# A two-layer linear-attention transformer on one core: the second layer's output weights spaced out, its attention chain moved up

## The chip, the core and the metric

The kernel runs on one core of one Trainium2 chip. The metric is the device time of one launch in microseconds, as the median of several runs. The engines are TensorE (PE; its weight loads are PEld), VectorE (DVE), ScalarE (ACT), GpSimd (POOL) and SyncE (SP), which issues most of the DMAs.

## The reference

A stack of four blocks works on x of 2048 x 576: attention, feed-forward, attention, feed-forward, with the same weights both times.

```python
x = x + A(layernorm(x))       # 32 heads of 18: phi = [softmax(p), softmax(-p)] with p = head @ w_phi,
                              # o = phi_q (phi_k^T v) / (phi_q . sum(phi_k) + 1e-6), then o @ wo
x = x + B(layernorm(x))       # relu(x @ w1 + b1)**2 @ w2 + b2, width 4608
x = x + A(layernorm(x))
x = x + B(layernorm(x))
```

All is float32. The kernel keeps that precision by splitting each matmul operand into a high and a low part and adding three products.

## The kernel before

The 2048 rows are worked in four blocks of 512 (0 to 3), and a block's feed-forward (`g_mlp`) is one **stage**. A stage runs over 36 slices of the hidden width. One slice is one **unit**: the hidden product H(f) (L955, 14 matmuls into `m_*ph`), relu and square on ACT (L960, L961), a cast and a subtraction on DVE that give the two parts `m_*hb` (L964, L965), and the second product S(f) (L980 and L972, 15 matmuls into `m_*acc`). On PE the order is H(f), S(f-1), H(f+1), S(f). The weights of a unit come from memory on SP's queue: `m_*h` (640 KB, for H) and `m_*s` (576 KB, for S), each with two buffers, so that the load of H(f+1) can go out when H(f-1) has ended.

Beside a stage runs the attention of the block that comes next (`plan_attend`). In the second layer the blocks come in the order 1, 0, 3, 2: block 0's attention (tiles `a_0*`) runs beside stage 1 (`m_1*`), block 3's beside stage 0, block 2's beside stage 3. For a block, the steps are:

- projections of the queries (`a_*qp`, L498) from activations fetched back from memory (`a_*uh`, `a_*ul`, L485); block 0 has its queries already,
- for each of four row tiles the softmaxes on DVE and ACT (L534 to L571), a rearrangement on POOL, a store to memory (L737), a fetch of it in another layout (L742, on ACT's queue), and a **flip**: a transpose in blocks on DVE (L747),
- ten copies in two parts (`pieces`, L756 and L757) and ten `times` steps of three matmuls each (`a_*pn`, L776),
- the output weights in four **pieces** o0h, o0l, o1h, o1l (L315 on SP, each as two DMAs of 126 and 72 rows). They go into the buffers of the fetched tiles (tag names `wraw` and `rr`), so they must wait for the last copies out of these,
- the projections with them (`a_*po`, L799), one row tile after another, then the norm, stored, fetched and flipped in the same manner for the next stage.

The order of all this is a table: `plan.put(turn, depth, call)` puts a call into a slot, two slots to a unit, and `weave` takes one slot after each H and one after each S. PE, ACT, DVE and POOL keep the order so written; the order on SP's queue is set by the framework's scheduler from when it thinks an operand is there. Every queue runs in order: an instruction that waits holds those behind it.

Of the kernel before, what the change touches and what calls it, by code (L numbers as in the profile page):

```python
# [21 lines left out]
def layers_kernel(  # L22
# [23 lines left out]
    out = out.rearrange("o s d -> (o s) d")  # L46
# [8 lines left out]
    NG = (H + HG - 1) // HG  # L55
# [39 lines left out]
    def weave(main, other, rate):  # L95

        due = 0.0
        for _ in main:
            due += rate
            while due >= 1.0 and next(other, other) is not other:  # L100
                due -= 1.0
        drain(other)
# [204 lines left out]
    def asked(which, name, tags=TAGS_A):  # L307

        pair, calls = [], []

        def ask(half, k):
            if k == 0:
                pair.append(piece_tiles(f"{name}{which}{half}", tags))
            for d, piece in moved(which, half, k, pair[half][k]):
                nc.sync.dma_start(piece, d)  # L315

        return pair, [lambda half=half, k=k: ask(half, k) for half in range(2) for k in range(2)]
# [163 lines left out]
    def unspill(b, x, i, name):  # L481
        if not x:
            x.update(xt_tiles(name))
        d, piece = xt_part(b, x, i)
        nc.sync.dma_start(piece, d)  # L485
# [38 lines left out]
    def make_raw(x, t, pair, name):  # L524
        raw = new_raw(t, name)
        for half in range(2):
            half_raw(x, t, pair, half, raw, name)
        return raw
# [280 lines left out]
    def plan_norm(plan, norm, x_of, stats, scales, turns, rests, late=()):  # L809
        for t in range(NT):  # L810
            plan.put(stats[t], 0, lambda t=t: norm.stats(t, x_of(t)))
            plan.put(scales[t], 1, norm.scale, t)
            plan.put(turns[t], -1 if t in late else 2, norm.turn, t)
        for h in range(2):
            plan.put(rests[h], 2, norm.rest, h)

    def plan_queries(plan, at, gap, layer, raws, er, ph, name):

        zb = sums[layer]["zb"]
        r = {}  # L820

        def first(t):
            if t == 0:
                r[0] = sb.tile([P, NT, 2, H], F32, tag="rq", name=f"{name}r", bufs=1)
            er.append(exponents(raws[t], f"{name}Q{t}"))

        def second(t):
            e, rt = er[t], r[0][:, t]
            totals(e, rt)
            m = sb.tile([P, 2, D], F32, tag="m", name=f"{name}m{t}", bufs=1)  # L830
            u = sb.tile([P, 2, H], F32, tag="u", name=f"{name}u{t}", bufs=1)
            nc.vector.tensor_mul(m, e, zb)
            nc.vector.tensor_reduce(u, m.rearrange("p s (h d) -> p s h d", d=DH), op=ALU.add, axis=AX.X)
            r[t + 1] = u

        def third(t):
            e, rt, u = er[t], r[0][:, t], r.pop(t + 1)
            nc.vector.tensor_mul(u, u, rt)
            nc.vector.scalar_tensor_tensor(u[:, 0], u[:, 0], DEN_EPS, u[:, 1], op0=ALU.add, op1=ALU.add)
            nc.vector.reciprocal(u[:, 1], u[:, 0])  # L840
            nc.vector.tensor_mul(rt, rt, u[:, 1].unsqueeze(1).to_broadcast([P, 2, H]))
            scaled(e, rt)
            ph.append(e)

        for t in range(NT):
            plan.put(at + gap * t, 0, first, t)
            plan.put(at + gap * t + 1, 1, second, t)
            plan.put(at + gap * t + 2, 2, third, t)
        return at + gap * (NT - 1) + 2

    def plan_attend(plan, at, gap, layer, b, raws, dst, name, o, queries=None):

        out = Out(layer, b, [], name)
        out.pair, calls = o
        if queries:
            for t in range(NT):
                plan.put(at + gap * t, 0, queries, t)
            at += 1
        if layer == 0:
            for n, call in enumerate(calls):  # L860
                plan.put(at + n, 9, call)
        done = at + 2
        at = plan_queries(plan, at, gap, layer, raws, [], out.ph, name) + 1
        if layer:
            for t in range(NT):
                for k, (step, call) in enumerate(((0.5, out.arrange), (1.5, out.store), (2.5, out.fetch), (4, out.flip))):
                    plan.put(done + gap * t + step, -1, call, t)
            at += 3.5
        for i in range(2 * NG):
            plan.put(at + i / 2, 0, out.pieces if layer else out.turn, i)  # L870
            plan.put(at + (i + 1 + layer) / 2, 1, out.times, i)
        if layer:
            for n, call in enumerate(calls):
                plan.put(at + NG + n / 4, 9, call)
            at += 1.5
        at += NG + 1
        for t in range(NT):
            plan.put(at + t - 1, 9, out.load, t)
        trips = range(NT) if layer else range(NT - 1)
        norm = TripNorm(dst, f"{name}n", b, out.keep, trips, layer == 1)  # L880
        more = 0 if queries else 2
        scales = [at + 1, at + 2, at + 3, at + 4 if layer else at + 5.5 + more]
        turns = [at + more + k for k in (4, 5, 6.5, 7)]
        for t in trips:
            plan.put(scales[t] + 0.5, -1, norm.store, t)
            plan.put(at + more + t + 2.5, -1, norm.fetch, t)
            plan.put(at + more + (3.5, 4.5, 6, 6.5)[t], -1, norm.flip, t)
        plan_norm(plan, norm, out.project, [at + t for t in range(NT)], scales, turns, [at + 5 + more, at + 7 + more])
# [538 lines left out]
    def body():  # L1427

        order = [NB - 1, NB - 2] + list(range(NB - 2))
        queries, other, o, last_keys = opening()  # L1430
        for layer in range(2):
            q1 = None
            ready, prev_rows, keep = {}, None, {}
            for i, b in enumerate(order):
                n = f"{layer}_{b}"
                nxt, rows = {}, []
                gen = g_mlp(layer, b, ready, rows, f"m{n}", layer == 0 and i == 0, i == 0, layer == 1 and i == NB - 1)
                plan = Plan()
                if i == 0:
                    out = Out(layer, b, [], f"t{layer}o")  # L1440
                    out.pair = o[0]
                    barrier(layer, b, last_keys, queries, other, ready, out, gen)
                    for t in range(NT):
                        plan.on(2 + t, 0, out.keep, t, out.x[t])
                at = 0
                if prev_rows is not None:
                    at = plan_keys(plan, prev_rows, i == NB - 1, keep)
                if i + 1 < NB:
                    nb, n2 = order[i + 1], f"a{layer}_{order[i + 1]}"
                    if i or layer:  # L1450
                        o = asked("o", n2, TAGS_C)
                    if i == 0:
                        plan_attend(plan, 1, 3, layer, nb, [other.raws[t] for t in range(NT)], nxt, n2, o)
                    else:
                        raws2, held = [], {}
                        start, step = (at - 4, 0.5) if at else (0, 0.75)
                        for k in range(4):
                            plan.put(start + 2 * step * k, -2, lambda k=k, held=held, nb=nb, n2=n2:
                                     unspill(nb, held, k, f"{n2}u"))
                        if q1 is None or not layer:  # L1460
                            q1, calls = asked("q", n2)
                            for call, k in zip(calls, (1, 3, 6, 7)):
                                plan.put(start + step * k, -3, call)
                        plan_attend(plan, at or 6.5, 2, layer, nb, raws2, nxt, n2, o,
                                    lambda t, held=held, q1=q1, raws2=raws2, n2=n2:
                                    raws2.append(make_raw(held, t, q1, f"{n2}q")))
                weave(gen, plan.slots(), 1.0)
                ready = nxt
                if layer == 0:
                    prev_rows = (b, rows)  # L1470
            if layer == 0:
                queries, other, o, last_keys = between(rows, keep)
                order = [order[-1], order[-2]] + order[:2]
# [43 lines left out]
    with tc.manual_schedule(engines=ordered):  # L1517
        body()
# [22 lines left out]
```

## Time and profile before

| | |
|---|---|
| Median of three runs | 2523.01 us (2520.92 to 2524.05) |
| The profiled execution | 2526.71 us, of which its span 2525.0 us |
| PE busy | 2495.7 us, 99% of the span |
| DVE, ACT, POOL busy | 1223.7, 769.7 and 152.5 us |
| DMA | 540.99 MB, 214 GB/s in the mean |
| TensorE's granted clock | 0.996 in the mean |

PE is busy nearly throughout; the other engines and the DMA work in its shadow, and count where PE waits for them. The page's table of waits and the timelines around them tell where that is.

### The profile page before, as it was taken

What the parts mean: (1) busy time and instruction counts of PE and PEld (TensorE: products, weight loads), DVE (VectorE), ACT (ScalarE), POOL (GpSimd) and SP (SyncE); (2) the same over time, 40 slices, a digit from 0 to 9 for tenths busy, and PEclk for the clock granted to TensorE, in tenths of its full rate; (3) what the DMA queues carried; (4) which work ended last, traced back from release to release, by engine and by line L of the source; (5) the groups of instructions that cost most, each with busy time, mean ns of one, the idle gap of its engine ahead of it and who ended that gap; (6) DMA issues with size and microseconds to landing.
All of it is one profiled execution on the core that took longest, in us unless ns stands there. A gap on an engine that the chain in (4) does not pass through costs nothing.

```text
span 2525.0 us, 37453 instructions
## 1 busy us (share of the span) xinstructions
PE 2495.7 (99%) x15084; PEld 2198.6 (87%) x15084; DVE 1223.7 (48%) x2115; ACT 769.7 (30%) x1358; POOL 152.5 (6%) x419
## 2 busy tenths in 40 slices
PE   9999999999999999999999999999999999999999
PEld 8998888898888988888889988788887888888887
DVE  6887955444635446355114776433463426433112
ACT  5544443322222222223223332313223222312221
POOL 4302000000000000000000011000010002000000
PEclk9999999999999999999999999999999999999999
DMA  9514888867648576484564348668575767667665
GB/s 318 175 53 135 288 279 283 307 230 268 215 157 288 179 255 207 165 292 146 193 196 158 130 139 268 215 196 281 177 254 181 259 225 239 206 204 247 197 195 171
DMA packets 196619, 540.99 MB, mean 214 GB/s; under 512 B 26270, under 2 KB 79390, under 8 KB 196446
## 3 DMA queue, kind: packets, MB, share of 16 engines
q1 hardware_dynamic: 163806, 511.06, 60.8%
q10 hardware_dynamic: 32640, 27.53, 3.4%
q8 instruction: 120, 1.97, 0.3%
q14 instruction: 53, 0.43, 0.0%
HBM read 440.12 MB, written 98.40 MB: 213 GB/s over the span
## 4 chain that ended last, share of the span: by engine, by line
PE 97%; DMA 2%; DVE 1%; ACT 0%; issue 0%; SPq 0%; DVEq 0%; ACTq 0%
PE m_2ph L955 9%; PE m_0ph L955 9%; PE m_1ph L955 9%; PE m_3ph L955 9%; PE m_2acc L980 7%; PE m_1acc L980 7%; PE m_3acc L980 7%; PE m_0acc L980 7%; PE m_2acc L972 2%; PE m_1acc L972 2%; PE m_0acc L972 2%; PE m_3acc L972 2%; PE a_0po L799 1%; PE a_2po L799 1%; PE kvp L598 1%; PE a_3po L799 1%
## 5 line engine op out<-in xcount | busy, mean ns | idle before, releaser
L955 PE MATMUL m_0ph<-a_0nh,m_0h 128*128 128x512 f32 x720 | 226.8, 397 | 5.6 <-DMA m_0h<-dw 5.6
L955 PE MATMUL m_2ph<-a_2nh,m_2h 128*128 128x512 f32 x720 | 225.4, 395 | 0.0
L980 PE MATMUL m_1acc<-m_1s,m_1hb 128*128 128x448 f32 x864 | 189.0, 367 | 0.4 <-PE m_1ph L955 0.4
L980 PE MATMUL m_2acc<-m_2s,m_2hb 128*128 128x448 f32 x864 | 189.3, 367 | 0.0
L980 PE MATMUL m_3acc<-m_3s,m_3hb 128*128 128x448 f32 x864 | 188.9, 367 | 0.3 <-DVE m_3hb L964 0.3
L980 PE MATMUL m_0acc<-m_0s,m_0hb 128*128 128x448 f32 x864 | 189.0, 367 | 0.0
L964 DVE CAST m_2hb<-m_2hr 128x512 fp32r<-128x512 f32 x72 | 30.8, 427 | 311.1 <-ACT m_2hr L961 310.7
L980 PEld LDWEIGHTS m_1acc<-m_1s,m_1hb 128*128 128x128 f32 x864 | 161.9, 188 | 18.7 <-PE m_1ph L955 0.5
L980 PEld LDWEIGHTS m_3acc<-m_3s,m_3hb 128*128 128x128 f32 x864 | 161.2, 188 | 17.4 <-PE m_3ph L955 0.5
L980 PEld LDWEIGHTS m_2acc<-m_2s,m_2hb 128*128 128x128 f32 x864 | 160.9, 188 | 16.1
L980 PEld LDWEIGHTS m_0acc<-m_0s,m_0hb 128*128 128x128 f32 x864 | 160.5, 188 | 15.4
L955 PEld LDWEIGHTS m_0ph<-a_0nh,m_0h 128*128 128x128 f32 x720 | 136.1, 189 | 37.4 <-issue 6.2
L964 DVE CAST m_0hb<-m_0hr 128x512 fp32r<-128x512 f32 x72 | 30.8, 428 | 273.4 <-ACT m_0hr L961 273.0
L955 PEld LDWEIGHTS m_2ph<-a_2nh,m_2h 128*128 128x128 f32 x720 | 135.3, 188 | 30.4
L960 ACT ACTIVATE m_0hr<-m_0ph,b1t 128x512 f32<-128x512 f32 x72 | 49.6, 689 | 353.9 <-PE m_0ph L955 343.8
L964 DVE CAST m_1hb<-m_1hr 128x512 fp32r<-128x512 f32 x72 | 30.7, 427 | 260.7 <-ACT m_1hr L961 260.7
L960 ACT ACTIVATE m_2hr<-m_2ph,b1t 128x512 f32<-128x512 f32 x72 | 49.6, 689 | 346.5 <-PE m_2ph L955 346.5
L960 ACT ACTIVATE m_1hr<-m_1ph,b1t 128x512 f32<-128x512 f32 x72 | 49.6, 689 | 324.5 <-PE m_1ph L955 314.4
L960 ACT ACTIVATE m_3hr<-m_3ph,b1t 128x512 f32<-128x512 f32 x72 | 49.6, 689 | 263.4 <-PE m_3ph L955 263.4
L964 DVE CAST m_3hb<-m_3hr 128x512 fp32r<-128x512 f32 x72 | 30.7, 426 | 197.7 <-ACT m_3hr L961 197.7
L955 PE MATMUL m_1ph<-t1onh,m_1h 128*128 128x512 f32 (+1 forms) x380 | 114.2, 387 | 5.6 <-DMA m_1h<-dw 4.9
L955 PE MATMUL m_3ph<-a_3nh,m_3h 128*128 128x512 f32 x360 | 114.7, 401 | 4.4 <-DMA m_3h<-dw 4.4
(1992 smaller groups left out, 5686.6 us busy)
## 6 DMA issues: line engine op xcount, KB each, us to landing
m_2h<-dw SPq DMA_DIRECT2D x72, 640.0 KB
m_0h<-dw SPq DMA_DIRECT2D x72, 640.0 KB
m_1h<-dw SPq DMA_DIRECT2D x72, 640.0 KB
m_2s<-dw SPq DMA_DIRECT2D x72, 576.0 KB
m_0s<-dw SPq DMA_DIRECT2D x72, 576.0 KB
m_1s<-dw SPq DMA_DIRECT2D x72, 576.0 KB
dw<-m_3h SPq DMA_DIRECT2D x36, 640.0 KB
m_3h<-dw SPq DMA_DIRECT2D x36, 640.0 KB
```

Source lines behind the costliest of these rows:

```text
L598: nc.tensor.matmul(po[32 * q : 32 * q + 32, :, j], vt[:, h * VW : h * VW + 32], e[:, :, h * DH : (h + 1) * DH], start=not stay, stop=True, ...
L799: nc.tensor.matmul(pt[:, :HP], a, m[:w, g], start=(g == 0 and k == 0), stop=(g == NG - 1 and k == 2))
L955: nc.tensor.matmul(ph[:, cols], a, m, start=(k == 0), stop=(k == 3 * KC + 1))
L960: nc.scalar.activation(hr, ph, AF.Relu, bias=b1t[:, f : f + 1])
L964: nc.vector.tensor_copy(hh, hr)
L972: nc.tensor.matmul(acc[KC], a, m, start=(f == 0 and k == 0), stop=(f == NF - 1 and k == 2))
L980: nc.tensor.matmul(acc[t][:, :R], a[:, rows], m, start=(f == 0 and k == 0), stop=(f == NF - 1 and k == 2))
```

## The change

Some numbers of the table change in the second layer. The four pieces are asked for in steps of 0, 1, 1.5 and 2.5 units instead of 0, 0.25, 0.5 and 0.75, and the projections begin 12 units behind the queries' last step instead of 11 (3 + 3 + 6 instead of 3.5 + 1.5 + 6). Flips and what follows them up to the pieces come half a unit earlier. For blocks 3 and 2 the whole chain begins 1.5 units earlier (turn 5 instead of 6.5), with the loads ahead of it placed closer together.

```diff
-                for k, (step, call) in enumerate(((0.5, out.arrange), (1.5, out.store), (2.5, out.fetch), (4, out.flip))):
+                for k, (step, call) in enumerate(((0.5, out.arrange), (1.5, out.store), (2.5, out.fetch), (3.5, out.flip))):
                     plan.put(done + gap * t + step, -1, call, t)
-            at += 3.5
+            at += 3
...
         if layer:
             for n, call in enumerate(calls):
-                plan.put(at + NG + n / 4, 9, call)
-            at += 1.5
+                plan.put(at + NG + (0, 1, 1.5, 2.5)[n], 9, call)
+            at += 3
         at += NG + 1
...
-                        start, step = (at - 4, 0.5) if at else (0, 0.75)
+                        start, step = (at - 4 if at else 0), 0.5
...
-                        plan_attend(plan, at or 6.5, 2, layer, nb, raws2, nxt, n2, o,
+                        plan_attend(plan, at or 5, 2, layer, nb, raws2, nxt, n2, o,
```

What stands in a row on SP in stage 1 around the pieces, before (the number behind `m_1h_` and `m_1s_` is the unit):

```order
L930 DMA m_1s_22_15722<-dw_22_191 128x1152
L315 DMA a_0o0h<-kept_oh 126x1152
L315 DMA a_0o0h<-kept_oh 72x288
L315 DMA a_0o0l<-kept_ol 126x1152
L315 DMA a_0o0l<-kept_ol 72x288
L315 DMA a_0o1h<-kept_oh 126x1152
L930 DMA m_1s_23_15785<-dw_23_192 128x1152
L315 DMA a_0o1h<-kept_oh 72x288
L315 DMA a_0o1l<-kept_ol 126x1152
L315 DMA a_0o1l<-kept_ol 72x288
L918 DMA m_1h_24_15800<-dw_24_157 128x1280
```

and after the change:

```order
L315 DMA a_0o0h<-kept_oh 126x1152
L930 DMA m_1s_22_15737<-dw_22_191 128x1152
L315 DMA a_0o0h<-kept_oh 72x288
L315 DMA a_0o0l<-kept_ol 126x1152
L315 DMA a_0o0l<-kept_ol 72x288
L918 DMA m_1h_24_15794<-dw_24_157 128x1280
L930 DMA m_1s_23_15790<-dw_23_192 128x1152
L315 DMA a_0o1h<-kept_oh 126x1152
L315 DMA a_0o1h<-kept_oh 72x288
L918 DMA m_1h_25_15838<-dw_25_158 128x1280
L930 DMA m_1s_24_15836<-dw_24_193 128x1152
L315 DMA a_0o1l<-kept_ol 126x1152
```

All four pieces stood ahead of the load for unit 24; now two stand ahead of it, one ahead of unit 25's and one ahead of unit 26's. Stages 0 and 3 show the same picture.

On DVE in stage 1, from the last cast ahead of block 0's last flip, before:

```order
L964 CAST m_1hb_15379<-m_1hr_15376 128x512
L965 TENSOR_TENSOR m_1hb_15379<-m_1hr_15376,m_1hb_15379 128x512
L747 STREAM_TRANSPOSE a_0e_15340<-a_0e_15340 128x1280
L964 CAST m_1hb_15420<-m_1hr_15417 128x512
L965 TENSOR_TENSOR m_1hb_15420<-m_1hr_15417,m_1hb_15420 128x512
L757 TENSOR_TENSOR a_0fl_15424<-a_0e_14882,a_0fh_15423 126x4x32
L757 TENSOR_TENSOR a_0fl_15424<-a_0e_15039,a_0fh_15423 126x4x32
```

and after:

```order
L964 CAST m_1hb_15379<-m_1hr_15376 128x512
L965 TENSOR_TENSOR m_1hb_15379<-m_1hr_15376,m_1hb_15379 128x512
L747 STREAM_TRANSPOSE a_0e_15340<-a_0e_15340 128x1280
L757 TENSOR_TENSOR a_0fl_15401<-a_0e_14882,a_0fh_15400 126x4x32
L757 TENSOR_TENSOR a_0fl_15401<-a_0e_15039,a_0fh_15400 126x4x32
L757 TENSOR_TENSOR a_0fl_15401<-a_0e_15196,a_0fh_15400 126x4x32
L757 TENSOR_TENSOR a_0fl_15401<-a_0e_15340,a_0fh_15400 126x4x32
L964 CAST m_1hb_15430<-m_1hr_15427 128x512
```

The flip keeps its place there, and the first copies now follow it at once, ahead of the next cast. On ACT the copies they depend on likewise stand ahead of the next relu. The other three flips of a block stand behind a cast in the same way.

On PE in stage 0, where block 3's query projections begin, before (the number behind `m_0h_` or `m_0s_` is the unit):

```order
L955 MATMUL m_0ph_16883<-a_0nl,m_0h_7_16841 128x512
L955 MATMUL m_0ph_16883<-a_0nh,m_0h_7_16841 128x512 x3
L498 MATMUL a_3qp_16905<-a_3q0h,a_3uh 128x288
L498 MATMUL a_3qp_16905<-a_3q0l,a_3uh 128x288
L498 MATMUL a_3qp_16905<-a_3q0h,a_3ul 128x288
L498 MATMUL a_3qp_16905<-a_3q0h,a_3uh 128x288
```

and after:

```order
L980 MATMUL m_0acc_16649<-m_0s_4_16754,m_0hb_16780 128x448 x3
L972 MATMUL m_0acc_16650<-m_0hb_16780,m_0s_4_16754 128x512 x3
L498 MATMUL a_3qp_16842<-a_3q0h,a_3uh 128x288
L498 MATMUL a_3qp_16842<-a_3q0l,a_3uh 128x288
L498 MATMUL a_3qp_16842<-a_3q0h,a_3ul 128x288
L498 MATMUL a_3qp_16842<-a_3q0h,a_3uh 128x288
```

The first projection stood behind H(7) and stands behind S(4) now, so H(6), S(5) and H(7) come after it.

## Prediction

> **What bounds the kernel now.** I read the page's head first, then the waits of TensorE, then its timeline at the three longest of them, then the SP queue there.
>
> ```profile
> span 2525.0 us, 37453 instructions
> PE 2495.7 (99%) x15084; PEld 2198.6 (87%) x15084; DVE 1223.7 (48%) x2115; ACT 769.7 (30%) x1358; POOL 152.5 (6%) x419
> ```
>
> TensorE (PE) is busy for 99% of the span, and the change neither adds nor removes a matmul. So it can only win or lose where PE waits. Of the waits of PE (total, times, longest) the first three are these; the rest of the list has nothing above 0.5 us outside the opening:
>
> ```profile
> PE m_0ph L955 <- DMA m_0h<-dw: 5.6, 1, 5.6
> PE m_1ph L955 <- DMA m_1h<-dw: 4.9, 1, 4.9
> PE m_3ph L955 <- DMA m_3h<-dw: 4.4, 1, 4.4
> ```
>
> One wait in each of the three stages that carry an attention block in the second layer, each for a first-weight load (`m_*h`). PE's timeline there, for each the last group before the wait, the first matmul after it, and the first matmul after that hidden product (start, duration):
>
> ```profile
> 1635.29 0.84 PE L972 MATMUL m_1acc<-m_1hb,m_1s 128*128 128x512 f32 x3
> 1641.06 0.77 PE L955 MATMUL m_1ph<-t1onh,m_1h 128*128 128x512 f32 x1 [4.92 <-DMA m_1h<-dw]
> 1646.67 2.60 PE L980 MATMUL m_1acc<-m_1s,m_1hb 128*128 128x448 f32 x12
> ...
> 1936.30 0.84 PE L972 MATMUL m_0acc<-m_0hb,m_0s 128*128 128x512 f32 x3
> 1942.77 0.76 PE L955 MATMUL m_0ph<-a_0nh,m_0h 128*128 128x512 f32 x1 [5.63 <-DMA m_0h<-dw]
> 1947.76 0.29 PE L799 MATMUL a_3po<-a_3o0h,a_3oh 126*128 126x288 f32 x1
> ...
> 2211.92 0.84 PE L972 MATMUL m_3acc<-m_3hb,m_3s 128*128 128x512 f32 x3
> 2217.13 0.76 PE L955 MATMUL m_3ph<-a_3nh,m_3h 128*128 128x512 f32 x1 [4.37 <-DMA m_3h<-dw]
> 2223.09 0.29 PE L799 MATMUL a_2po<-a_2o0h,a_2oh 126*128 126x288 f32 x1
> ```
>
> A hidden product (H), a second product (S) and a `times` step without a stall, in the chain (start, us), and stretches of the core (busy us of each engine with counts, granted clock, DMA share, GB/s):
>
> ```profile
> 1584.46 3.26 PE m_1ph L955 x14
> 1587.71 2.46 PE m_1acc L980 x12
> 1590.18 0.70 PE m_1acc L972 x3
> ...
> 1594.10 0.69 PE a_0pn L776 x3
> ```
>
> ```profile
> 575.00:600.00 25.00, 25.00 (x363) 21.48 (x363) 13.45 (x19) 7.19 (x11) 0.00 (x0) 1.00 0.97 356
> 1624.00:1640.00 16.00, 12.13 (x56) 9.76 (x54) 3.45 (x7) 3.23 (x5) 0.00 (x0) 0.98 0.93 267
> 1642.00:1646.00 4.00, 4.00 (x11) 3.08 (x10) 0.00 (x0) 0.00 (x0) 0.00 (x0) 0.50 0.14 54
> ```
>
> So H takes 3.26 and S 3.16, a unit 6.4 us. After each wait the clock is granted at 0.50 and H takes far longer. The price of one wait is the late start (against the end of S, its last group's start + 0.70) and the slow H: 1641.06 - 1635.99 = 5.07 and 5.61 - 3.26 = 2.35; 5.77 and 4.99 - 3.26 = 1.73; 4.51 and 5.96 - 3.26 = 2.70. Together **7.4 + 7.5 + 7.2 = 22.1 us**. The Trainium skill, "TensorE: Matmul & The Clock Gate", Part 1, says that the array falls to half rate after about one idle window of 3.4 us; the 0.50 agrees. By it a leftover wait under that length would cost itself alone.
>
> Why the load is late stands in the SP queue of the first stage, with sizes from the issue view:
>
> ```profile
> 1621.32 0.32 SPq L930 DMA_DIRECT2D m_1s<-dw  x1
> 1623.66 0.76 SPq L315 DMA_DIRECT2D a_0o0h<-kept_oh  x2
> ...
> 1629.07 0.34 SPq L930 DMA_DIRECT2D m_1s<-dw  x1
> ...
> 1629.94 0.74 SPq L315 DMA_DIRECT2D a_0o1l<-kept_ol  x2
> 1630.74 0.35 SPq L918 DMA_DIRECT2D m_1h<-dw  x1
> ```
>
> ```profile
> m_1h<-dw SPq DMA_DIRECT2D x24, 640.0 KB
> m_1s<-dw SPq DMA_DIRECT2D x23, 576.0 KB
> a_0o0h<-kept_oh SPq DMA_DIRECT2D x1, 567.0 KB
> a_0o0h<-kept_oh SPq DMA_DIRECT2D x1, 81.0 KB
> ```
>
> All four pieces (4 x 648 KB) are issued from 1623.66 to 1630.7, ahead of the `m_1h` that PE needs at 1635.99. Its buffer is free when H(22) ends, at 1635.99 less S, H, S and two `times`, about 1625; it goes out at 1630.74 and is used at 1641.06, 10.3 us later.
>
> **The change, part by part.** No instruction is added.
>
> *Pieces spaced.* In the new order a piece or two stands between weight loads, and each `m_*h` follows the piece only by one. A load issued at the end of H(f-1) is needed at H(f+1): S + H + S = 9.6 us. I queue the bytes in order at 267 GB/s, the row above, in which just these transfers run (m_h 655 kB, m_s 590, piece 664). Counted back from 1635.99, where the new order falls in step with the old, H(22) ends at 1625.7 and H(23) at 1632.8. o0h goes out at about 1621.6, an estimate: 2 us before the 1623.66 above, since the last copies out of its buffer come half a unit earlier but behind a relu and square on ACT. Ahead of m_1h of unit 24, issued at 1625.7, then are 664 + 590 + 664 less 4.1 us x 267 = 823 kB; with its own 655 that is 5.5 us of 10.3 allowed (one `times` of 0.7 lies in it). Ahead of unit 25's, issued at 1632.8: 1478 + 590 + 664 less 7.1 x 267 = 836 kB, 5.6 us of 9.6: the tightest. Unit 26's: 6.3 us, with a projection's 30 matmuls more to go before it is needed. The same sum for the old stalled load gives a landing at 1638.3 where it was used at 1641.06, so 2.75 us are missing in it (completion, sharing with the two loads behind); with these the tightest still has 9.6 - 5.6 - 2.75 = **1.25 us** to spare. S loads have more. So I put what is left of the stalls at 0, with bounds of 0 and 3 us per stage (rivals). The last piece lands about 1645; the projections start one S and one H behind where they did, at about 1649, so they don't wait.
>
> One rule speaks against this. The Trainium skill, "DMA: Bandwidth & Descriptors", section "Why a DMA increments its semaphore by 16 and not by 1", says a transfer uses the largest count of engines up to 16 that divides its rows: 14 for a piece's 126 rows, 12 for its 72. An estimate by that page: a piece loads the busiest engines like 774 kB instead of 664, and the spare time falls from 1.25 to about 0, still no wait. 267 GB/s in stretches with pieces against 356 in the first one agrees in direction; as it was measured with pieces in it, most of the rule is already in my sum.
>
> *Flips half a unit earlier.* VectorE's block transposes wait for a fetch; here the last two of the first stage (ACT's queue, then DVE with a softmax step of another block first, then ACT):
>
> ```profile
> 1556.63 0.34 ACTq L742 DMA_DIRECT2D a_0e<-phs  x1
> ...
> 1577.80 0.34 ACTq L742 DMA_DIRECT2D a_0e<-phs  x1
> ```
>
> ```profile
> 1526.38 0.75 DVE L534 TENSOR_REDUCE a_0Q2m<-t1pqs 128x32 f32<-128x576 f32 x1
> ...
> 1564.68 1.50 DVE L747 STREAM_TRANSPOSE a_0e<-a_0e 128x1280 f32<-128x1280 f32 x1
> ...
> 1583.21 0.69 DVE L965 TENSOR_TENSOR m_1hb<-m_1hr,m_1hb 128x512 fp32r<-128x512 f32 x1
> 1586.07 1.51 DVE L747 STREAM_TRANSPOSE a_0e<-a_0e 128x1280 f32<-128x1280 f32 x1 [2.17 <-DMA a_0e<-phs]
> ```
>
> ```profile
> 1587.75 0.69 ACT L960 ACTIVATE m_1hr<-m_1ph,b1t 128x512 f32<-128x512 f32 x1 [5.04 <-PE m_1ph L955]
> ...
> 1595.39 1.13 ACT L756 ACTIVATE a_0fh<-a_0e 126x128 fp32r<-126x128 f32 x4
> ```
>
> The last fetch landed 8.27 us after issue. In the new order every flip stands like this one, right behind a cast, so DVE waits some 2 us and is busy 1.5 with it. What follows on DVE is then late: four softmax steps of 0.7, and the next cast. A cast has 3.8 us of play: the one that ends at 1583.90 is used when the H of 1584.46 ends, at 1587.72. The first copies for `times` (L756) now stand on ACT between the last flip and L960: the flip ends at 1587.58, one copy takes 0.3, so L960 starts at 1587.9 instead of 1587.75, and the next H needs the bank that it frees 3 us later (S and `times`, 3.85, less its 0.69). Cost 0, covered by those 3 to 3.8 us; each us beyond them would be PE's.
>
> *Chain 1.5 units up (blocks 3 and 2).* Its projections read activations that must be back from memory:
>
> ```profile
> 1753.03 0.42 SPq L485 DMA_DIRECT2D a_3ul<-xtl  x1
> ```
>
> ```profile
> 1784.36 0.29 PE L498 MATMUL a_3qp<-a_3q0h,a_3uh 128*128 128x288 f32 x1
> ```
>
> They move ahead of H, S, H = 9.7 us, to 1774.7. Even landing as slowly as the stalled load (10.3 us) the data is there at 1763.4. SP's order up to there is the same. Cost 0.
>
> *Block 0 ends one unit later.* Its last copies move to about two units before the stage's end; blocks 3 and 2 had theirs in the last unit, and the three rows of waits above hold none for them. Cost 0.
>
> Sum: -22.1 us. The profiled execution took 2526.71 (span 2525.0 + 1.7), which gives 2504.6; it lies 3.7 above the median of the runs shown, and for that median 2523.01 - 22.1 = **2501**.
>
> **Rivals.** (1) *The transfers are only spread and the volume still bounds.* Three units carry 4 x 664 + 3 x 1245 = 6390 kB, 23.9 us at 267 GB/s, and PE needs 19.9. Without the prefetch's play each stage pays 4 us: 2501 + 12 = 2513. For it: share 0.93. Against: the 9.6 us of play, and 25 us at share 0.97 and 356 GB/s with PE at 25.00. (2) *The stall isn't removed*, because PE then waits for the `m_*s` or for the pieces themselves at the projections: 2523. Against: the last piece has 3 us to spare. (3) *Slower: fetches late at the flips.* Twelve flips now hold DVE, and four-block copies hold ACT, ahead of what frees PE. If a fetch lands 2.8 us later than the 8.27 above, PE starts to wait; from 5.0 us later (13.3 us), 12 x 2.3 = 27 us eat the gain and 0.2% more: 2529. Against: the fetch of 1556.63 was flipped 8.05 us after issue without a wait.
>
> **How the numbers follow.** All stalls gone, 2501: 0.70. Rival 1, wholly or in part, 2504 to 2513: 0.16. Rival 2: 0.07. Rival 3: 0.07. The range 2497 to 2511 takes the first and most of the second, its lower end the spread of the runs and the 3.7 us above. 0.2% (5 us) is about what a measurement of this kernel can tell: faster 0.86, same 0.07, slower 0.07.
>
> **What would show it.** Right: the three DMA rows gone from PE's waits, clock 1.00 around the pieces, H at 3.26 there, SP's `m_*h` issued within 0.5 us of H's end, span near 2503. Rival 1: waits of 1 to 4 us for `m_*h` in units 24 to 28. Rival 3: PE waiting for `m_*hb` or ACT behind L747. Wrong at all: a fresh wait in the last units of a stage.

## The result, and the profile after

The changed kernel takes **2505.3 us** (median of four runs, 2504.81 to 2505.67) against 2523.14 for the kernel before beside it: ratio 0.9927, 95% interval 0.9912 to 0.9943. In a second set of five runs it took 2504.8 against 2523.6: 0.9924, 0.9911 to 0.9938. So about 18 us are gone, where 22.1 were forecast for the time of 2501. The profiled execution took 2505.67 us.

The head of the page, the first waits of TensorE with the one `m_*h` row of the second layer, and that wait in the timeline, which is its only one of 0.2 us or more after 1500 us:

```profile
span 2503.9 us, 37459 instructions
PE 2490.2 (99%) x15084; PEld 2196.3 (88%) x15084; DVE 1226.1 (49%) x2115; ACT 770.8 (31%) x1358; POOL 153.9 (6%) x419
```

```profile
PE warm L1308 <- POOL ident L124: 1.5, 1, 1.5
...
PE m_3ph L955 <- DMA m_3h<-dw: 0.3, 1, 0.3
```

```profile
2011.08 0.47 PE L955 MATMUL m_3ph<-a_3nh,m_3h 128*128 128x512 f32 x1 [0.26 <-DMA m_3h<-dw]
```

The waits of 5.6, 4.9 and 4.4 us are gone; the 0.26 stands before H(2) of stage 3, far from any piece. The SP queue around the pieces in stage 1, the chain there, and two windows (the columns as before):

```profile
1622.70 0.33 SPq L315 DMA_DIRECT2D a_0o0h<-kept_oh  x1
...
1626.98 0.34 SPq L918 DMA_DIRECT2D m_1h<-dw  x1
1630.82 0.34 SPq L930 DMA_DIRECT2D m_1s<-dw  x1
1631.25 0.78 SPq L315 DMA_DIRECT2D a_0o1h<-kept_oh  x2
1634.08 0.34 SPq L918 DMA_DIRECT2D m_1h<-dw  x1
```

```profile
1623.73 3.21 PE m_1ph L955 x14
...
1630.79 3.27 PE m_1ph L955 x14
...
1643.53 3.26 PE m_1ph L955 x14
```

```profile
1624.00:1640.00 16.00, 16.00 (x73) 13.38 (x72) 2.84 (x5) 3.12 (x5) 0.00 (x0) 1.00 0.96 306
1642.00:1646.00 4.00, 4.00 (x20) 3.31 (x19) 0.94 (x2) 0.00 (x0) 0.00 (x0) 1.00 1.00 302
```

H(22) ends at 1626.94 (1623.73 + 3.21) and its buffer's next load goes out at 1626.98. In the kernel before, H(22) ended at 1625.20 and the same load went out at 1630.74, 5.5 us later. Every H shown takes 3.2 to 3.3 us, the clock stays at 1.00, and TensorE has no gap there.

### The profile page after: what moved, and what is told of

It is laid out like the page before. It is cut to its first block, busy times and chain, and to the rows that moved or that the text cites. A ratio compares the mean times of both kernels' runs of the same rounds, so it can differ in the third digit from the quotient of the medians.

```text
span 2503.9 us, 37459 instructions
## 1 busy us (share of the span) xinstructions
PE 2490.2 (99%) x15084; PEld 2196.3 (88%) x15084; DVE 1226.1 (49%) x2115; ACT 770.8 (31%) x1358; POOL 153.9 (6%) x419
## 4 chain that ended last, share of the span: by engine, by line
PE 97%; DMA 1%; DVE 1%; ACT 0%; issue 0%; DVEq 0%; SPq 0%; ACTq 0%
PE m_0ph L955 9%; PE m_1ph L955 9%; PE m_2ph L955 9%; PE m_3ph L955 9%; PE m_1acc L980 7%; PE m_0acc L980 7%; PE m_2acc L980 7%; PE m_3acc L980 7%; PE m_1acc L972 2%; PE m_0acc L972 2%; PE m_2acc L972 2%; PE m_3acc L972 2%; PE a_0po L799 1%; PE a_2po L799 1%; PE kvp L598 1%; PE a_3po L799 1%
## 5 line engine op out<-in xcount | busy, mean ns | idle before, releaser
L955 PE MATMUL m_3ph<-t0onh,m_3h 128*128 128x512 f32 (+1 forms) x380 | 113.1, 384 | 0.6 <-ACT t0onh L390 0.5
L955 PE MATMUL m_0ph<-a_0nl,m_0h 128*128 128x512 f32 x288 | 113.1, 393 | 0.0
```

Source lines behind the costliest of these rows:

```text
L955: nc.tensor.matmul(ph[:, cols], a, m, start=(k == 0), stop=(k == 3 * KC + 1))
```

## The experiments

Each is the changed kernel or the one before with a part put back or altered. Ratios are to the kernel before on the same chip.

| Kernel | Median, us (lowest to highest, runs) | Ratio, 95% interval |
|---|---|---|
| spacing alone | 2520.27 (2518.99 to 2522.55, 11) | 0.9989 (0.9980 to 0.9998) |
| chain and flips alone | 2522.94 (2521.70 to 2526.38, 11) | 0.9999 (0.9991 to 1.0008) |
| projections early | 2515.59 (2511.10 to 2518.33, 5) | 0.9965 (0.9952 to 0.9978) |
| pieces on GpSimd's queue | 2509.94 (2509.44 to 2513.58, 5) | 0.9948 (0.9935 to 0.9962) |
| chain back | 2517.63 (2515.59 to 2522.27, 11) | 0.9982 (0.9973 to 0.9991) |
| flips late | 2508.51 (2506.71 to 2512.48, 5) | 0.9949 (0.9935 to 0.9963) |
| half spacing | 2511.52 (2510.21 to 2515.55, 5) | 0.9960 (0.9948 to 0.9973) |
| changed kernel again | 2504.80 (2504.47 to 2505.20, 5) | 0.9924 (0.9911 to 0.9938) |

**Chain and flips alone** (the changed kernel with the pieces together again):

```diff
-                plan.put(at + NG + (0, 1, 1.5, 2.5)[n], 9, call)
-            at += 3
+                plan.put(at + NG + n / 4, 9, call)
+            at += 1.5
```

> The changed kernel with the pieces together again (steps of a quarter of a unit, projections 1.5 units behind as before); flips half a unit earlier and the chain 1.5 units up remain. Theory: all four pieces again stand ahead of the m_*h load of one unit on SP, so three waits of 4 to 6 us with the slow clock behind them, 2523 within 3. Rival (the chain's or the flips' move gives the gain by itself): 2505. If flips half a unit earlier cost something that the spacing covers, it ends above 2526.

Measured: no change in time (2522.9), as the theory said, and the three waits of PE are there as in the kernel before:

```profile
PE m_3ph L955 <- DMA m_3h<-dw: 5.9, 1, 5.9
PE m_1ph L955 <- DMA m_1h<-dw: 3.9, 1, 3.9
PE m_0ph L955 <- DMA m_0h<-dw: 3.5, 1, 3.5
```

The moves of chain and flips are worth nothing without the spacing.

**Spacing alone** (the kernel before with the two lines of the pieces changed):

```diff
-                plan.put(at + NG + n / 4, 9, call)
-            at += 1.5
+                plan.put(at + NG + (0, 1, 1.5, 2.5)[n], 9, call)
+            at += 3
```

> The kernel before with the pieces alone spaced at 0, 1, 1.5 and 2.5 units and the projections behind them; flips and the chain of blocks 3 and 2 stay where they were, so the attention of a block ends 2.5 units (for blocks 3 and 2) or one and a half later than before, in the last unit of its stage or at its end. Theory (the order of the weight loads on the SP queue is the whole cause): the three waits of 4.4 to 5.6 us for m_*h are gone here as after the change, 2505, unless the late end shows: then TensorE waits at the start of the next stage for the block's last copies, 1 to 8 us in each of two stages, 2508 to 2518, and this is what moving the chain up was for. Rival (the gain comes from the chain and the flips): the three waits stay, 2523.

Measured: 2520.3, between the two ranges. (With this edit all three blocks end 1.5 units later, blocks 3 and 2 too, not 2.5.) The three `m_*h` waits are gone, and two new ones stand where stages 3 and 2 begin. PE's waits, its timeline at the first of them, and the same place of the changed kernel (first row: the stage's last matmuls; last row: the new stage's first S):

```profile
PE m_3ph L955 <- ACT a_3nh L456: 4.0, 1, 4.0
PE m_2ph L955 <- ACT a_2nh L456: 3.6, 1, 3.6
```

```profile
2000.37 1.48 PE L980 MATMUL m_0acc<-m_0s,m_0hb 128*128 128x448 f32 x6
2005.83 0.50 PE L955 MATMUL m_3ph<-a_3nh,m_3h 128*128 128x512 f32 x1 [3.98 <-ACT a_3nh L456]
2007.22 0.80 PE L955 MATMUL m_3ph<-a_3nl,m_3h 128*128 128x512 f32 x1 [0.88 <-DVE a_3nl L457]
...
2015.10 2.63 PE L980 MATMUL m_3acc<-m_3s,m_3hb 128*128 128x448 f32 x12
```

```profile
1999.75 1.47 PE L980 MATMUL m_0acc<-m_0s,m_0hb 128*128 128x448 f32 x6
...
2007.54 2.60 PE L980 MATMUL m_3acc<-m_3s,m_3hb 128*128 128x448 f32 x12
```

From first to last row it is 14.73 us against 7.79, so this wait with its slow clock costs 6.9; the other, by the same rows 2275.34 to 2290.43, costs 7.3. These 14.2 us eat most of what the spacing brings. What ends last there is the block's own new input (L442, L456, L457), and on DVE it stands behind the additions that close the old stage (L1046, L1049). At the first place its last two transposes also wait for their fetches, 0.26 and 0.96 us; at the second they don't. Rows of the second place:

```profile
2274.58 1.23 DVE L1046 TENSOR_TENSOR m_3x<-m_3acc,m_3x 128x448 f32<-128x448 f32 x2 [1.31 <-PE m_3acc L980]
2275.73 0.87 DVE L1049 TENSOR_TENSOR m_3x<-m_3py,m_3x 128x128 f32<-128x128 f32 x4
2276.52 1.14 DVE L1046 TENSOR_TENSOR m_3x<-m_3acc,m_3x 128x448 f32<-128x448 f32 x2
2277.59 1.06 DVE L457 TENSOR_TENSOR a_2nl<-a_2nn,a_2nh 128x512 fp32r<-128x512 f32 x1
```

**Chain back** (the changed kernel, chain of blocks 3 and 2 at its old place, flips still half a unit earlier):

```diff
-                        start, step = (at - 4 if at else 0), 0.5
+                        start, step = (at - 4, 0.5) if at else (0, 0.75)
...
-                        plan_attend(plan, at or 5, 2, layer, nb, raws2, nxt, n2, o,
+                        plan_attend(plan, at or 6.5, 2, layer, nb, raws2, nxt, n2, o,
```

> The changed kernel with the chain of blocks 3 and 2 put back to turn 6.5 and the loads ahead of it in their old steps; spacing and the flips half a unit earlier remain. With the spacing alone (2520.3) TensorE waited at the start of stages 3 and 2 for the last copies, 4.9 and 4.0 us, worth 6.9 and 7.3 with the slow clock behind. Theory (the end of the block is what counts, each half unit of 3.2 us earlier takes as much off that wait): 3.2 of each wait go, 0.7 to 1.7 stay, no slow clock: 2506 to 2510. Rival (the last fetches, not the place of the copies, end last): the waits shrink by under 1 us, 2516 to 2520.

Measured: 2517.6, by the number in the rival's range, but not by its mechanism: at neither place does a copy or transpose on DVE wait for a fetch here. The half unit of 3.2 us took 2.8 us off the wait at the start of stage 3 (4.9 to 2.1) and only 0.6 off that of stage 2 (4.0 to 3.4, of which 0.6 for the high part, L456), and a clock below 1.00 stayed behind both. By the rows used for the spacing alone the two places cost 4.0 and 5.5 us (2000.39 to 2012.14 and 2274.55 to 2287.85, less 7.79). PE's waits:

```profile
PE m_2ph L955 <- DVE a_2nl L457: 2.8, 1, 2.8
PE m_3ph L955 <- DVE a_3nl L457: 2.1, 1, 2.1
```

They are now for the last L457, which again stands behind L1046 and L1049 on DVE (2000.15 to 2003.1 us at the first place). That group waits for the stage's last matmuls, so what stands behind it is late however early its fetch is; the copies must stand in front of it. In the changed kernel the 1.5 units put them there: its last L457 starts at 1993.49, before DVE's last cast of the stage. (This version also waits 1.3 us for an `m_0s` at the end of stage 0, which is not explained here, and 1.6 for an `m_3h` beside the pieces, which is taken up under the next version.)

**Flips late** (the changed kernel, flips and what follows up to the pieces at the old place, projections and chain as changed):

```diff
-                for k, (step, call) in enumerate(((0.5, out.arrange), (1.5, out.store), (2.5, out.fetch), (3.5, out.flip))):
+                for k, (step, call) in enumerate(((0.5, out.arrange), (1.5, out.store), (2.5, out.fetch), (4, out.flip))):
...
-            at += 3
+            at += 3.5
...
-            at += 3
+            at += 2.5
```

> The changed kernel with flips, copies, times steps and pieces half a unit later, as before the change; projections and the chain 1.5 units up stay. Theory (flips half a unit earlier cost and gain nothing by themselves; the pieces still have a unit between them): no wait for m_*h; the last piece now goes out half a unit nearer to its projection, so a wait there of 0 to 1 us per stage: 2505 to 2508. Rival (the half unit at the flips carries part of the gain, or the last pieces come late): 2509 to 2515.

Measured: 2508.5, between the two ranges, with runs up to 2512.5. The profile is of the run of 2506.71. The chain in stage 0:

```profile
1913.65 10.02 DMA m_0h<-dw
1923.66 0.14 issue
1923.80 3.49 PE m_0ph L955 x14
```

This load (unit 27's, as the attention lies otherwise in stage 0) has the place that unit 25's has in stage 1, which I had called the tightest. It goes out at H's end, lands 10.0 us later and is late by 0.7; no wait for a piece is seen. On SP the piece o0l now goes out behind the load ahead of this one (1906.22 after 1905.83), so that two pieces, not one, stand between the two loads. The traces of spacing alone, chain back and this version have this order at six places, and the load is late at two of them, here and by 1.6 us in chain back (stage 3, 11.05 us to landing). With the order of the changed kernel, at nine places (all six of its two profiles, the other two of spacing alone, the other one of chain back), it is never late. So the half unit at the flips carries a part of the gain, some 3 us at the median, with the order on SP as the likely cause. The profile also has a wait of 1.4 us for `m_3h` before H(2) of stage 3. No profile shows the runs above 2508; their mean granted clock was 0.998 to 0.999 instead of 1.000, so the clock probably fell behind a longer wait.

**Half spacing** (the changed kernel with pieces at 0, 0.5, 1, 1.5):

> The changed kernel with the pieces at 0, 0.5, 1 and 1.5 units instead of 0, 1, 1.5 and 2.5; all else as changed. Three pieces now stand ahead of one m_*h load. By the sum of the prediction (267 GB/s, bytes in order) that load has 664 kB more ahead of it, 2.5 us, against 1.25 us spare: a wait of about 1 us per stage, no slow clock, 2507 to 2510. If the transfers run at the 300 GB/s seen after the change: no wait, 2505. Rival (blocking of SP behind a piece that waits for its buffer counts, not bytes): waits of 3 us and more, 2512 to 2520.

Measured: 2511.5, between the two ranges. In the profile, of the fastest run (2510.2), PE waits 2.2, 1.4 and 1.7 us for `m_*h` without a slow clock (H 3.45), twice my estimate at the worst place. The chain of stage 1 shows why: H(22), a `times` step and S(21) end, and then the load for unit 24 is reached through the SP queue:

```profile
1622.98 3.21 PE m_1ph L955 x14
...
1630.07 0.34 SPq L930
...
1630.46 0.38 SPq L315
...
1630.89 7.55 DMA m_1h<-dw
```

Its buffer was free at 1626.2, but it stood behind an `m_1s` whose own buffer came free only with the S that ended at 1630.05, and behind the second half of a piece: 4.7 us late on the queue. In the sum I had counted only bytes, and the rival had the queue blocked by a piece, not by a weight load. The order table above shows that the kernel before had the same `m_1s_23` ahead of its load, with that `m_1s` issued at 1629.07: the pieces had pushed `m_1h` behind a weight load that was needed later and could not start.

**Pieces on GpSimd's queue** (the kernel before; nothing but the queue of the second layer's pieces changes):

```diff
-                nc.sync.dma_start(piece, d)
+                queue.dma_start(piece, d)
...
-                        o = asked("o", n2, TAGS_C)
+                        o = asked("o", n2, TAGS_C, nc.gpsimd if layer else nc.sync)
```

> The kernel before, with the second layer's pieces issued on GpSimd's DMA queue instead of SP's, at their old time, all four within less than one unit. The same bytes pass in the same stretch, but no weight load on SP stands behind a piece. Theory A (what counts is the order on SP: weight loads queued behind pieces that wait for their buffers): m_*h goes out within 0.5 us of its H's end and the waits are gone or under 2 us, 2503 to 2509. Theory B (rival 1 of the prediction, the volume: 2.6 MB of pieces fill the DMA engines in that stretch, in whatever order they are issued): m_*h is issued in time but lands late, with waits of 2 to 5 us, 2512 to 2523. If the pieces hold GpSimd's other work, a wait for a_*oh or a_*pn shows.

Measured: 2509.9, between the two theories' ranges. Stage 1 has no wait; stages 0 and 3 keep 2.3 and 1.0 us. Stage 0's SP queue and chain, the issue view with the median us to landing, and a window:

```profile
1920.87 0.32 SPq L918 DMA_DIRECT2D m_0h<-dw  x1
```

```profile
1920.87 12.35 DMA m_0h<-dw
1933.21 0.14 issue
1933.35 3.45 PE m_0ph L955 x14
```

```profile
a_3o0h<-kept_oh POOLq DMA_DIRECT2D x1, 567.0 KB, 7.3
a_3o1l<-kept_ol POOLq DMA_DIRECT2D x1, 567.0 KB, 16.8
```

```profile
1925.00:1930.00 5.00, 5.00 (x24) 4.29 (x23) 0.60 (x2) 1.32 (x2) 0.00 (x0) 1.00 1.03 252
```

The load goes out in time and still needs 12.35 us, at a DMA share of 1.03, with four pieces in flight beside it; the last piece needs 16.8. So 13.2 of the 18 us go when the pieces leave SP's queue, and the other 5, of which these two waits are 3.3, need the pieces apart in time. Leaving the queue takes away both the wait behind an `m_*s` and the pieces' bytes ahead of the load; no run parts these two. The Trainium skill, "DMA: Bandwidth & Descriptors", section "Issuing engines are not separate DMA queues", says that DMAs started by different engines run on the same 16 DMA engines and interleave; these rows agree.

**Projections early** (the changed kernel with `at += 1.5` behind the pieces instead of 3):

> The changed kernel with the projections 1.5 units earlier, so that they begin about when the last piece is issued. Theory of the prediction: the m_*h waits stay away, but TensorE now waits for the last pieces at the first projection, since a piece needs 2 to 5 us from issue to landing: one wait of 2 to 8 us per stage in three stages, with the slow clock behind those over 3 us, 2511 to 2530. Rival (the shift of the projections is not needed, pieces land in time): 2505 and no wait.

Measured: 2515.6 at the median, in the theory's range; the profile is of the fastest of the five runs, 2511.1:

```profile
1643.74 0.40 PE L799 MATMUL a_0po<-a_0o1l,a_0oh 126*128 126x288 f32 x1 [2.23 <-DMA a_0o1l<-kept_ol]
1926.39 0.40 PE L799 MATMUL a_3po<-a_3o1l,a_3oh 126*128 126x288 f32 x1 [1.63 <-DMA a_3o1l<-kept_ol]
...
2196.72 0.40 PE L799 MATMUL a_2po<-a_2o1l,a_2oh 126*128 126x288 f32 x1 [0.77 <-DMA a_2o1l<-kept_ol]
```

The projections do need their later place: the last piece takes 5.6 to 7.1 us in these three chains, longer than the 2 to 5 I had expected, and is waited for. No wait of this profile has a slow clock behind it. It also has 1.3 us for an `m_3h` before H(2) of stage 3.

**The kernel before once more, and the changed kernel once more:**

> The kernel before, profiled once more, to see how much of its spread (2520 to 2528 in 21 runs) lies in the three waits. Theory: the rest of the kernel takes 2505 in every run, and the price of the three waits with the slow clock behind makes up the difference, 15 to 22 us: time less price comes out at 2504 to 2506, as for the first profile (2526.7 - 22.1). Rival: the spread lies elsewhere, and the three waits again cost 22 in a run near 2523.

Measured: 2521.67 us in this execution, with shorter waits. Its waits, PE's timeline at the one in stage 1 (the last group before it, the first matmul after it, the first behind that hidden product), and the hidden product behind the wait in stage 3:

```profile
PE m_0ph L955 <- DMA m_0h<-dw: 3.6, 1, 3.6
PE m_1ph L955 <- DMA m_1h<-dw: 3.6, 1, 3.6
PE m_3ph L955 <- DMA m_3h<-dw: 2.7, 1, 2.7
```

```profile
1636.36 0.84 PE L972 MATMUL m_1acc<-m_1hb,m_1s 128*128 128x512 f32 x3
1640.83 0.76 PE L955 MATMUL m_1ph<-t1onh,m_1h 128*128 128x512 f32 x1 [3.62 <-DMA m_1h<-dw]
1646.84 2.60 PE L980 MATMUL m_1acc<-m_1s,m_1hb 128*128 128x448 f32 x12
```

```profile
2214.72 3.46 PE m_3ph L955 x14
```

Priced as in the prediction, the late start plus what H takes over 3.26, the wait in stage 1 costs 1640.83 - 1637.06 = 3.77 and 6.01 - 3.26 = 2.75, together 6.5; the one in stage 0 costs 6.6 and, with the clock still at 1.00, the one in stage 3 costs 2.9. That is 16.1, and 2521.67 - 16.1 = 2505.6. The theory holds: the kernel before is 2505 to 2506 plus three waits of varying length.

> The changed kernel once more, for its spread. Theory: what differs from run to run in the kernel before (2519.5 to 2527.7) is the length of three waits and the clock behind them; the changed kernel has no such wait, so its runs lie within 2 us of 2505. Rival (half a microsecond to spare in one stage is not enough in every run): some runs at 2507 to 2512, with a wait of 0.5 to 2 us for an m_*h load, as the versions with three pieces ahead of a load or with flips half a unit later show.

Measured: five runs within 0.7 us, and no `m_*h` wait in the second layer above 0.2 us. The kernel before spread over 8.8 us in nine runs beside them. The rival is not seen in these nine runs of the changed kernel, four of the first set and five of this.

## Why the prediction was right, and where it was off

- *Three waits for `m_*h` are the whole price.* Shown. They stand in all versions with the pieces together on SP, at 2.7 to 5.9 us; in the others a wait for `m_*h` is 2.3 at most or absent. The two profiles of the kernel before give 2504.6 and 2505.6 when the waits are taken out. The agreement is closer if one counts from the matmul in stage 1 that waits 0.47 us for ACT (at 1481.17, 1482.26 and 1482.26 us) to the end of the span: 1021.7 us without the waits in both profiles of the kernel before, and 1021.6 in the changed kernel.
- *The sum, -22.1.* Right for the execution it was read in: 2504.6 against 2505.3. The step that failed is the last one, where I took 22.1 from the median of other runs to get 2501. The price of the waits belongs to its own execution: 22.1 in one of 2526.71 us, 16.1 in one of 2521.67. The median run, near 2523, pays about 18. The time alone would not have told the forecast from rival 1, to which I had given 2504 to 2513; what tells them apart is that no wait for `m_*h` is left around the pieces.
- *What is left of the stalls: 0.* Right (0.26 us in one unrelated place). The issue times came out as worked out: o0h at 1622.70 and `m_1h` at 1626.98 and 1634.08 against 1621.6, 1625.7 and 1632.8, in a stage that began 1.1 us later.
- *1.25 us to spare for the tightest load.* Not borne out. With flips late its counterpart took 10.0 us where PE could spare 9.4 and the same sum, with its 2.75, would by my estimate give some 8; in the changed kernel it had 9.45 (1634.08 to 1643.53) and made it, by a margin no run shows. The transfers ran at 306 GB/s there instead of my 267, but the landing time varies more than the sum allows.
- *Flips half a unit earlier, cost 0.* Right on the cost, though the flips early also gain some 3 us, which I had not seen. I had read all flips as waiting some 2 us behind their cast; of the twelve, three waited, 2.43, 2.10 and 0.24 us. PE did not wait behind them, as rival 3 would have had it. The longest:

```profile
1868.05 1.51 DVE L747 STREAM_TRANSPOSE a_3e<-a_3e 128x1280 f32<-128x1280 f32 x1 [2.43 <-DMA a_3e<-phs]
```

- *Chain 1.5 units up, cost 0.* Right, and short: I didn't ask what happens without it. It is what keeps the late projections from running into the stage's end, worth 12 us (2517.6 against 2505; in the profile 9.5 of them stand at the two stage starts), and 15 together with the flips (2520.3). These sets ran on different chips, so the differences are rough. The rows of before held no wait there, because the projections were 1.5 units earlier than with the spacing alone.
- *Why the load was late.* Half told. I charged the pieces' bytes. The larger part, 13.2 of 18 us by the pieces on GpSimd's queue, hangs on SP's queue, which runs in order: the load could have gone out at 1625.20 and stood until 1629.07 behind a later-needed `m_1s` that waited for its buffer, and until 1630.74 behind that and the rest of the pieces. How much of the 13.2 is this wait and how much the bytes ahead on the queue, no run shows.
- *Rival 1, the volume.* Partly true: with the pieces off SP's queue but still together, 5 us were left, until the pieces were apart.

## What to carry to other kernels

A set of transfers that is moved into a busy stretch is judged twice: by what stands behind it on its queue, waits of its neighbours for buffers included, and by the bytes in that stretch. Spacing work out makes it end later, so look at what stands at the end before you claim the gain: here neither half of the change was worth 0.2%, and both together 0.7%. And take a stall's price off the execution in which you read it, not off a median.

## What the runs showed of the hardware

The clock's fall makes the price of a wait jump. A wait of 2.74 us (the kernel before once more) left it at 1.00 and H took 3.46; one of 3.49 (chain and flips alone) brought it to 0.50 afterwards, from 1927 to 1929 us, and H took 5.04. The Trainium skill, "TensorE: Matmul & The Clock Gate", Part 1, gives an idle window of about 3.4 us, free-running, so that the point varies; these two agree. One case does not fit a whole idle window. With the chain back, PE was idle for 2.1 us around 2003, after 4 us without a gap (and 1.3 idle before those), and the clock fell all the same (granted clock third from the right):

```profile
1999.00:2002.00 3.00, 3.00 (x17) 2.46 (x16) 2.94 (x9) 2.43 (x3) 0.00 (x0) 1.00 1.03 421
2002.00:2004.00 2.00, 0.10 (x1) 0.00 (x0) 2.00 (x4) 0.00 (x0) 0.00 (x0) 1.00 0.99 396
2004.00:2007.00 3.00, 2.81 (x7) 2.20 (x8) 0.76 (x2) 0.00 (x0) 0.00 (x0) 0.60 0.99 346
```

So a wait of 2 us is not safe from it. Why the clock fell behind this one, and not behind those of 2.2 us (half spacing), 2.3 (GpSimd's queue) and 2.74, stays open.
